# Converting a dense layer's float64 weights in place on ScalarE and VectorE

## The chip, the core and the metric

One core of a Trainium2 chip runs the kernel. The metric is the device time of one execution in microseconds (us), taken as the median of several runs. The engines are TensorE (PE, with its weight loads as PEld), VectorE (DVE), ScalarE (ACT), GpSimd (POOL) and SyncE (SP), which here only issues transfers.

## What is computed

Chunked attention with memory rows feeds a dense layer with a SiLU gate, and that feeds a routed layer of eight experts. The dense layer's weights are the part that the change touches. They are drawn without a cast, so they are float64, unlike q, k and v.

```python
def _moe_setup():
    n_tokens, d_model, d_ff = (3072, 512, 2048)
    return {'x': ..., 'w_in': np.random.randn(d_model, d_ff) * (1.0 / np.sqrt(d_model)), 'w_out': np.random.randn(d_ff, d_model) * (1.0 / np.sqrt(d_ff))}

def reference(**kwargs):
    attn_out = _attn_ref(**attn_kwargs)      # 4 batches, 8 heads, 768 rows, chunks of 32 with context
    x = np.ascontiguousarray(attn_out.transpose(0, 2, 1, 3)).reshape(B * S, H * D)
    h = x @ w_in                             # _moe_ref
    x = ((h * (1.0 / (1.0 + np.exp(-h)))) @ w_out).astype(np.float32)
    return _moe2_ref(x=x, **moe2_kwargs)     # gate, argmax expert, relu MLP of that expert
```

## The kernel before

The 3072 tokens are cut into 8 blocks j of 384; each is fed by four attention blocks n of 96 queries. The hidden width 2048 of the dense layer is cut into 16 slices f of 128. For each (j, f) TensorE forms `h{j}.{f}` (12 matmuls: three float32r passes over four column groups) and `y{j}.{f}` (9 matmuls: three passes for three groups of 128 tokens); between them ScalarE and VectorE do tanh, a multiplication, and a split into a high and a low part (`th`, `ts`, `gh`, `gl`; lines 558 to 561). The products of all f of block 0 come first, then block 1, and so on; `in_turn` keeps the order h, h, y, h, y.

The weights of a slice f are needed first by `h0.{f}`. So block 0 runs only as fast as slices are converted; from block 1 on the converted weights `wh` and `wl` (32 tiles of one pool tag "w" with 36 slots) stay in SBUF and are used again.

`conversion(f)` makes, for i = 0 (a slice of w_in) and i = 1 (a slice of w_out), from float64 words a float32 value and then two float32r parts. Each float64 is two 32-bit words, here called low and high. The units, with the engine that runs them:

- `c0_f` (SP, lines 467 and 469): the two loads into `wd{f}.0` and `wd{f}.1`. The w_in slice is 128 columns out of 2048, so each piece is 1 KB long in memory; those of w_out are 4 KB. It waits for `cb` of three slices before (`CONV_AHEAD`).
- `c1` (ACT; DVE for f = 0; lines 474, 476): high word, read as a float32, times 2^-112, into `wm`.
- `ca` (DVE, line 480): `wm` shifted left by three bits, both halves in one instruction of 1024 elements.
- `cs` (DVE, line 484): the sign of the high word put into `wm`.
- `cb` (DVE for f = 0, 3, ..., 15, line 489; else ACT, line 491): the top three bits of the low word, as an integer, into `wt`.
- `cl` (POOL, line 495): `wm` plus `wt`; this is the float32 value.
- `ch` (ACT, line 498): high part into `wh`.
- `c5` (line 502): `wm` minus `wh` into `wl`, on POOL for i = 0 and on DVE for i = 1.

All units are put in order once, when the program is built, by the list schedule of class `Plan`, from estimated lengths, ranks and free slots. On the chip each engine, and SP's queue of transfers, runs its own list strictly in that order and waits where something isn't there yet. So a load on SP that waits also holds back the loads of attention (`LQ`, `LK`, `LV`; lines 353, 359 to 361, 364) behind it.

Attention of the next blocks runs in between: scores `S` (PE, line 388), minima `M` (DVE, line 393), exponentials `E` (ACT, line 400), row sums and reciprocals `R` (DVE, lines 405 and 406), normalisation `N` (POOL, line 411, two instructions for each block n), transposes `X` (PE, line 415), copies `P` (line 418), values `V` (PE, line 423), and the split `H` and `L` (ACT line 426, DVE line 429). `h1.0` needs `L4` to `L7`.

Of the kernel before, what the change touches and what calls it, by code (L numbers as in the profile page):

```python
# [164 lines left out]
def kernel(  # L165
# [291 lines left out]
    def conversion(f):  # L457
        for i in range(2):
            T.new(f"wd{f}.{i}", "w", [P, DM, 2], I32)
        T.new(f"wm{f}", "w", [P, 2, DM])  # L460
# [3 lines left out]
        wd = [f"wd{f}.0", f"wd{f}.1"]

        def load():
            sp.dma_start(
                out=T[wd[0]].rearrange("p (c f) w -> p c (f w)", c=KD), in_=w_in[:, f * P:f * P + P].bitcast(I32).rearrange("(c p) x -> p c x", p=P))
            sp.dma_start(out=T[wd[1]].rearrange("p f w -> p (f w)"), in_=w_out[f * P:f * P + P, :].bitcast(I32))

        def scale_down(i):
            m, x = T[f"wm{f}"][:, i], T[wd[i]][:, :, 1].bitcast(F32)
            if f in D_C1:
                dve.tensor_scalar(out=m, in0=x, scalar1=2.0 ** -112, scalar2=None, op0=ALU.mult)
            else:
                act.activation(out=m, in_=x, func=AF.Copy, scale=2.0 ** -112)  # L476

        def shift():
            mi = T[f"wm{f}"].bitcast(I32)
            dve.tensor_scalar(out=mi, in0=mi, scalar1=3, scalar2=None, op0=ALU.logical_shift_left)  # L480
# [5 lines left out]
        def rest(i):
            t, x = T[f"wt{f}"][:, i], T[wd[i]][:, :, 0].bitcast(U32)
            if f in D_T1:
                dve.tensor_scalar(out=t, in0=x, scalar1=2.0 ** -29, scalar2=None, op0=ALU.mult)
            else:  # L490
                act.activation(out=t, in_=x, func=AF.Copy, scale=2.0 ** -29)
# [684 lines left out]
```

## Time and profile before

| what | value |
|---|---|
| three timed runs | 1021.09, 1023.49, 1030.64 us |
| their median | 1023.49 us |
| span of the profiled execution (first to last instruction) | 1021.5 us |
| time of the profiled execution outside its span | not recorded |
| PE busy, share of the span | 959.6 us, 94% |
| DVE / ACT / POOL busy | 724.1 / 479.0 / 218.2 us |
| moved by the DMA engines | 110.99 MB |

The profile lists an engine as busy while one of its instructions runs; neighbouring instructions of an engine can overlap by a few hundredths of a microsecond. A wait inside an instruction for something that is no semaphore is counted as its duration. The granted clock is a share of TensorE's 2.4 GHz.

### The profile page before, as it was taken

To read this page: it belongs to the slowest core of one execution; us is meant where nothing else is said; L and a number is where in the kernel's file an instruction comes from. 1 tells how busy PE (TensorE), PEld (TensorE's weight loads), DVE (VectorE), ACT (ScalarE), POOL (GpSimd) and SP (SyncE) were. 2 spreads that over 40 slices of the span, in tenths; PEclk is the share of its full clock that TensorE was granted. 3 is DMA by queue.
4 is the path that set the end of the run, shared out by engine and by line. 5 is a ranking of instruction groups with operands and counts; after the bars stand their busy time and mean duration, and the time that the engine had idled before them with its cause. 6 is when DMAs were issued, how large, how long until landed. Compare 5 with 4: busy or idle time off the path is not lost. (4 is left out here: it accounts for less than half of the span.)

```text
span 1021.5 us, 15964 instructions
## 1 busy us (share of the span) xinstructions
PE 959.6 (94%) x5356; PEld 847.6 (83%) x5356; DVE 724.1 (71%) x2031; ACT 479.0 (47%) x1273; POOL 218.2 (21%) x186
## 2 busy tenths in 40 slices
PE   6696899999999999999999999998999999999994
PEld 3575778889889889889889888997998888988983
DVE  5999988957966975984993993775975455544550
ACT  5666665626535544544553452224233344433541
POOL 6678552101201201111120210001012021112101
PEclk8789989999999999999999999999999999999998
DMA  9825421221231230221321211136057455456311
GB/s 285 271 77 169 132 70 50 89 90 50 78 101 30 82 117 20 81 89 42 99 72 59 88 43 42 42 101 218 22 179 232 153 169 176 138 163 208 129 49 44
DMA packets 99458, 110.99 MB, mean 109 GB/s; under 512 B 18623, under 2 KB 73695, under 8 KB 99360
## 3 DMA queue, kind: packets, MB, share of 16 engines
q1 hardware_dynamic: 95360, 96.96, 30.0%
q0 software_dynamic: 4000, 12.85, 3.8%
q8 instruction: 46, 0.75, 0.3%
q14 instruction: 52, 0.43, 0.1%
HBM read 97.20 MB, written 12.85 MB: 108 GB/s over the span
## 5 line engine op out<-in xcount | busy, mean ns | idle before, releaser
L411 POOL TENSOR_TENSOR pt<-pt,rs 96x512 f32<-96x512 f32 x64 | 83.8, 1328 | 411.7 <-DVE rs L406 332.3
L400 ACT ACTIVATE pt<-pt,mn 96x128 f32<-96x128 f32 x256 | 99.5, 392 | 42.6 <-DVE mn L393 42.5
L495 POOL TENSOR_TENSOR wm<-wm,wt 128x512 int32<-128x512 int32 x32 | 49.9, 1568 | 24.7 <-DVE wm L484 16.6
L400 ACT ACTIVATION_READ_ACCUMULATOR pt<-pt,mn 96x1 f32 x256 | 48.5, 190 | 0.0
L380 DVE TENSOR_TENSOR pad<-qk,pad 64x512 fp32r<-64x512 f32 x48 | 45.5, 947 | 0.7
L423 PE MATMUL pv<-px,v 128*64 128x96 f32 x512 | 30.9, 267 | 9.0 <-DVE mn L393 5.6
L423 PEld LDWEIGHTS pv<-px,v 128*64 128x64 f32 x512 | 24.5, 147 | 16.5 <-issue 12.7
L376 ACT CAST pad<-qk 64x512 fp32r<-64x512 f32 x48 | 29.5, 614 | 0.8 <-DMA qk<-in_k_dram 0.3
L502 POOL TENSOR_TENSOR wl<-wm,wh 128x512 fp32r<-128x512 f32 x16 | 24.8, 1548 | 5.2 <-ACT wh L498 5.2
L426 ACT CAST xh<-pv 128x384 fp32r<-128x384 f32 x32 | 15.1, 474 | 17.7 <-PE pv L423 17.7
L498 ACT CAST wh<-wm 128x512 fp32r<-128x512 f32 x32 | 19.6, 618 | 7.0 <-POOL wm L495 7.0
L393 DVE DVE_READ_ACCUMULATOR2_ANT mn<- 96x1 f32 x256 | 20.2, 79 | 0.0
L502 DVE TENSOR_TENSOR wl<-wm,wh 128x512 fp32r<-128x512 f32 x16 | 19.3, 1208 | 0.5 <-ACT wh L498 0.5
L480 DVE TENSOR_SCALAR wm<-wm 128x1024 int32<-128x1024 int32 x16 | 17.1, 1069 | 1.3 <-ACT wm L476 1.3
L890 POOL DMA_INDIRECT xge0.0_7148<-yd,gie x1 | 1.2, 1174 | 77.7 <-DMA rawxe0.1_7118<-in_moe_w_dram 77.7
L429 DVE TENSOR_TENSOR xl<-pv,xh 128x384 fp32r<-128x384 f32 x32 | 17.4, 547 | 0.0
L380 DVE TENSOR_TENSOR qs<-qk,qs 128x384 fp32r<-128x384 f32 x24 | 16.4, 682 | 0.5
L592 DVE DVE_READ_ACCUMULATOR2_ANT lg<- 128x1 f32 x192 | 15.7, 82 | 0.0
L376 ACT CAST qs<-qk 128x384 fp32r<-128x384 f32 x24 | 12.3, 512 | 0.2
L405 DVE TENSOR_SCALAR rs<-sm 96x8 f32<-96x8 f32 x32 | 9.6, 299 | 1.2 <-ACT pt L400 1.2
L632 DVE TENSOR_SCALAR ya<-ya,rg 128x512 f32<-128x512 f32 x16 | 7.4, 501 | 0.2
L406 DVE RECIPROCAL rs<-rs 96x8 f32<-96x8 f32 x32 | 6.4, 199 | 1.1
(6397 smaller groups left out, 3218.5 us busy)
## 6 DMA issues: line engine op xcount, KB each, us to landing
v<-in_v_dram SPq DMA_DIRECT2D x32, 256.0 KB, 2.7
qk<-in_k_dram SPq DMA_DIRECT2D x24, 256.0 KB, 3.2
qk<-in_q_dram SPq DMA_DIRECT2D x24, 192.0 KB, 3.3
yd<-ya SPq DMA_DIRECT2D x16, 256.0 KB, 2.1
pad<-in_k_dram SPq DMA_DIRECT2D x16, 128.0 KB, 3.9
yd<-yb SPq DMA_DIRECT2D x8, 256.0 KB, 2.5
qs<-in_q_dram SPq DMA_DIRECT2D x8, 192.0 KB, 4.5
wd0.0_114<-in_moe_w_in_dram SPq DMA_DIRECT2D x1, 512.0 KB
```

What stands on the lines that cost most here:

```text
L376: act.copy(out=to[0], in_=x)
L380: dve.tensor_tensor(out=to[1], in0=x, in1=to[0].bitcast(F32), op=ALU.subtract)
L393: dve.tensor_tensor_reduce(out=T[f"pt{n}"][:, h, :], in0=T[f"sc{n}.{i // 2}"][:, h % 4, :], in1=mask, scale=-scale, scalar=3.0e38, op0=ALU ...
L400: act.activation(out=pt[:, h, :], in_=pt[:, h, :], func=AF.Exp, bias=T[f"mn{n}"][:, h:h + 1], scale=-1.0, accum_out=T[f"sm{n}"][:, h:h + 1])
L411: pool.tensor_tensor(out=pt[:, half, :], in0=pt[:, half, :], in1=bc(T[f"rs{n}"][:, half], [QB, 4, P]), op=ALU.mult)
L423: pe.matmul(T[f"pv{n}"][r:r + 64, h // 2, :], T[f"v{n}"][:, D * h:D * h + D], T[f"px{n}"][:, h, :], start=True, stop=True)
L429: dve.tensor_tensor(out=T[f"xl{j}"][:, :, cols], in0=T[f"pv{n}"], in1=T[f"xh{j}"][:, :, cols].bitcast(F32), op=ALU.subtract)
L480: dve.tensor_scalar(out=mi, in0=mi, scalar1=3, scalar2=None, op0=ALU.logical_shift_left)
L495: pool.tensor_tensor(out=mi, in0=mi, in1=T[f"wt{f}"][:, i], op=ALU.add)
L498: (dve.tensor_copy if f in D_CH else act.copy)(out=T[f"wh{f}"][:, i], in_=T[f"wm{f}"][:, i])
L502: e.tensor_tensor(out=T[f"wl{f}"][:, i], in0=T[f"wm{f}"][:, i], in1=T[f"wh{f}"][:, i].bitcast(F32), op=ALU.subtract)
L592: dve.tensor_tensor_reduce(out=part(products), in0=part(y_at[t]), in1=T[f"wg{j}.{e // 2}"][:, e % 2], scale=1.0, scalar=0.0, op0=ALU.mult, ...
```

## The change

The host lays both weights out so that slice f is one block of 128 partitions with 4 KB each, contiguous. The load of a slice is two units now, one for each i, and each waits for `cv` of the same i three slices before. The intermediate tiles `wm` and `wt` are gone; everything up to the float32 value happens inside `wd`, seen as four 16-bit pieces per float64 (0 and 1 of the low word, 2 and 3 of the high word):

- `ct` (DVE for f = 0, 3, ..., 15, else ACT): top three bits of the low word into piece 0, as a 16-bit integer;
- `cs` (DVE): the sign bit of piece 3 into piece 1, 16 bits wide;
- `c1` (ACT, always): high word times 2^-112, in place;
- `cv` (DVE): high word shifted left by three, or'ed with the low word, in place; this is the float32 value;
- `ch` (ACT): high part into `wh`, as before;
- `c5` (DVE, always): the low part into `wl`.

```diff
-D_T1 = range(0, 16, 3)
-D_LO = [(f, 1) for f in range(16)]
-D_C1 = (0,)
-D_CH = ()
+D_T = range(0, 16, 3)
...
-        T.new(f"wm{f}", "w", [P, 2, DM])
-        T.new(f"wt{f}", "w", [P, 2, DM], I32)
...
+        def load(i):
+            sp.dma_start(out=T[f"wd{f}.{i}"].rearrange("p f w -> p (f w)"), in_=(w_in, w_out)[i][f].bitcast(I32))
+        def halves(i):
+            return T[f"wd{f}.{i}"].bitcast(U16)
+        def rest(i):
+            to, x = halves(i)[:, :, 0], T[f"wd{f}.{i}"][:, :, 0].bitcast(U32)
+            if f in D_T:
+                dve.tensor_scalar(out=to, in0=x, scalar1=2.0 ** -29, scalar2=7.0, op0=ALU.mult, op1=ALU.min)
             else:
+                act.activation(out=to, in_=x, func=AF.Copy, scale=7.49 * 2.0 ** -32)
         def sign(i):
+            x = halves(i)
+            dve.tensor_scalar(out=x[:, :, 1], in0=x[:, :, 3], scalar1=2 ** 15, scalar2=None, op0=ALU.bitwise_and)
+        def exponent(i):
+            x = T[f"wd{f}.{i}"][:, :, 1].bitcast(F32)
+            act.activation(out=x, in_=x, func=AF.Copy, scale=2.0 ** -112)
         def whole(i):
-            mi = T[f"wm{f}"][:, i].bitcast(I32)
-            pool.tensor_tensor(out=mi, in0=mi, in1=T[f"wt{f}"][:, i], op=ALU.add)
+            x = T[f"wd{f}.{i}"]
+            dve.scalar_tensor_tensor(out=x[:, :, 1], in0=x[:, :, 1], scalar=3, in1=x[:, :, 0], op0=ALU.logical_shift_left, op1=ALU.bitwise_or)
         def low(i):
-            e = dve if (f, i) in D_LO else pool
-            e.tensor_tensor(out=T[f"wl{f}"][:, i], in0=T[f"wm{f}"][:, i], in1=T[f"wh{f}"][:, i].bitcast(F32), op=ALU.subtract)
+            dve.tensor_tensor(out=T[f"wl{f}"][:, i], in0=T[f"wd{f}.{i}"][:, :, 1].bitcast(F32), in1=T[f"wh{f}"][:, i].bitcast(F32), op=ALU.subtract)
...
-        U(f"c0_{f}", "SP", 2920, load, [f"cb_{f - CONV_AHEAD}.1" if f < KF - 2 else f"c5_{f - 2}.1", f"c0_{f - 1}"], wd, extra=DMA_LAG)
+            U(f"c0_{x}", "SP", 400, lambda i=i: load(i), [f"cv_{f - CONV_AHEAD}.{i}", f"c0_{f}.0" if i else f"c0_{f - 1}.1"], [wd], extra=DMA_LAG)
+            U(f"cs_{x}", "DVE", 370, lambda i=i: sign(i), [f"ct_{x}"], [wd], **C)
+            U(f"c1_{x}", "ACT", 600, lambda i=i: exponent(i), [f"cs_{x}"], [wd], **C)
+            U(f"ct_{x}", *(("DVE", 370) if f in D_T else ("ACT", 600)), lambda i=i: rest(i), [f"c0_{x}"], [wd], **C)
+            U(f"cv_{x}", "DVE", 610, lambda i=i: whole(i), [f"c1_{x}", f"ct_{x}"], [wd], **C)
+            U(f"ch_{x}", "ACT", 560, lambda i=i: high(i), [f"cv_{x}"], [wd, f"wh{f}"], **C)
+            U(f"c5_{x}", "DVE", 610, lambda i=i: low(i), [f"ch_{x}"], [wd, f"wh{f}", f"wl{f}"], **C)
...
+    if name == "moe_w_in":
+        return a.reshape(-1, P, a.shape[1] // P, P).transpose(2, 1, 0, 3).reshape(-1, P, a.shape[0])
+    if name == "moe_w_out":
+        return a.reshape(-1, P, a.shape[1])
```

## Rows read from the trace of the kernel before

**Rows 1.** The page, part 1: busy time, share of span, instructions by engine.

```profile
PE 959.6 (94%) x5356; PEld 847.6 (83%) x5356; DVE 724.1 (71%) x2031; ACT 479.0 (47%) x1273; POOL 218.2 (21%) x186
```

**Rows 2.** Windows: length, busy of each engine, granted clock, DMA share, GB/s.

```profile
200.00:300.00 100.00, 99.26 (x601) 88.53 (x601) 75.81 (x245) 47.20 (x137) 12.55 (x10) 1.00 0.24 77
...
39.10:151.10 112.00, 91.15 (x461) 76.05 (x460) 106.95 (x196) 73.18 (x192) 80.18 (x56) 0.91 0.42 132
8.40:147.00 138.60, 105.51 (x563) 86.07 (x564) 131.78 (x277) 92.74 (x258) 97.89 (x70) 0.86 0.53 166
0.00:39.10 39.10, 25.06 (x145) 16.61 (x145) 28.02 (x101) 24.51 (x85) 24.15 (x31) 0.78 0.91 273
```

**Rows 3.** Waits of PE, 39 to 151 us: total, times, longest.

```profile
PE yp0.0_506 L529 <- DVE gl0.5_799 L561: 3.4, 1, 3.4
```

**Rows 4.** Timeline of PE: start, length, first matmuls of h0.0 and of h1.0.

```profile
39.09 1.10 PE L521 MATMUL hp0.0_439<-xh,wh 128*128 128x384 f32 x4
...
151.15 0.86 PE L521 MATMUL hp1.0_1461<-xh,wh 128*128 128x384 f32 x4
```

**Rows 5.** Windows, 0 to 150, of lines 480, 484, 489, 502 in turn.

```profile
0.00:150.00 150.00, 17.10 (x16) 0.87 0.55 168
...
0.00:150.00 150.00, 37.61 (x32) 0.87 0.55 168
...
0.00:150.00 150.00, 7.66 (x12) 0.87 0.55 168
...
0.00:150.00 150.00, 19.33 (x16) 24.76 (x16) 0.87 0.55 168
```

**Rows 6.** The same of lines 561 and 405, both DVE.

```profile
0.00:150.00 150.00, 15.02 (x15) 0.87 0.55 168
...
0.00:150.00 150.00, 5.73 (x8) 0.87 0.55 168
```

**Rows 7.** The same of lines 495 and 411, both POOL.

```profile
0.00:150.00 150.00, 49.93 (x32) 0.87 0.55 168
...
0.00:150.00 150.00, 20.83 (x16) 0.87 0.55 168
```

**Rows 8.** Timeline of DVE: instructions of the shortest lengths that recur.

```profile
11.90 0.42 DVE L474 TENSOR_SCALAR wm<-wd0.0_114 128x512 f32<-128x512 f32 x1
12.24 0.42 DVE L474 TENSOR_SCALAR wm<-wd0.1_116 128x512 f32<-128x512 f32 x1
...
51.55 0.68 DVE L484 SCALAR_TENSOR_TENSOR wm<-wd4.0_371,wm 128x512 int32<-128x512 int32 x1
52.15 0.68 DVE L484 SCALAR_TENSOR_TENSOR wm<-wd4.1_373,wm 128x512 int32<-128x512 int32 x1
...
53.82 0.68 DVE L480 TENSOR_SCALAR wm<-wm 128x1024 int32<-128x1024 int32 x1
...
14.26 0.17 DVE L405 TENSOR_SCALAR rs<-sm 96x8 f32<-96x8 f32 x1
```

**Rows 9.** Timelines of DVE, then of POOL: instructions that ran side by side.

```profile
21.52 2.23 DVE L405 TENSOR_SCALAR rs<-sm 96x8 f32<-96x8 f32 x1
...
39.46 1.78 DVE L502 TENSOR_TENSOR wl<-wm,wh 128x512 fp32r<-128x512 f32 x1
...
22.46 1.26 POOL L495 TENSOR_TENSOR wm<-wm,wt 128x512 int32<-128x512 int32 x1
...
39.07 3.32 POOL L495 TENSOR_TENSOR wm<-wm,wt 128x512 int32<-128x512 int32 x2 [0.68 <-issue]
```

**Rows 10.** Windows, 0 to 150, of line 491, ACT.

```profile
0.00:150.00 150.00, 12.87 (x20) 0.87 0.55 168
```

**Rows 11.** Timeline of SP's queue: transfers issued.

```profile
49.13 0.46 SPq L469 DMA_DIRECT2D wd9.1_702<-in_moe_w_out_dram  x1
...
73.47 0.33 SPq L353 DMA_DIRECT2D qs<-in_q_dram  x1
73.91 0.38 SPq L467 DMA_DIRECT2D wd10.0_789<-in_moe_w_in_dram  x1
```

**Rows 12.** Timeline of DVE: the last split that h1.0 needs.

```profile
143.53 0.55 DVE L429 TENSOR_TENSOR xl<-pv,xh 128x384 fp32r<-128x384 f32 x1
```

More of the change, by code (lines that the diff above doesn't have):

```diff
@@ L13 @@
 I32 = mybir.dt.int32
+U16 = mybir.dt.uint16
 U32 = mybir.dt.uint32
@@ L187 @@
     NT, DM = out.shape
-    DFF = w_in.shape[1]
+    KF = w_in.shape[0]
     E, _, FE = w1.shape
     NMOD = m_bias.shape[0]
-    KF = DFF // P
     KE = FE // P
@@ L459, in conversion @@
             T.new(f"wd{f}.{i}", "w", [P, DM, 2], I32)
-        T.new(f"wm{f}", "w", [P, 2, DM])
-        T.new(f"wt{f}", "w", [P, 2, DM], I32)
         T.new(f"wh{f}", "w", [P, 2, DM], F32R)
         T.new(f"wl{f}", "w", [P, 2, DM], F32R)
[L464 to L474, printed above, removed]
-            else:
[L476 to L480, printed above, removed]
+        def load(i):
+            sp.dma_start(out=T[f"wd{f}.{i}"].rearrange("p f w -> p (f w)"), in_=(w_in, w_out)[i][f].bitcast(I32))
@@ L482, in sign @@
+        def halves(i):
[4 more added lines that the diff above has]
+                dve.tensor_scalar(out=to, in0=x, scalar1=2.0 ** -29, scalar2=7.0, op0=ALU.mult, op1=ALU.min)
+            else:
+                act.activation(out=to, in_=x, func=AF.Copy, scale=7.49 * 2.0 ** -32)
         def sign(i):
-            mi = T[f"wm{f}"][:, i].bitcast(I32)
-            dve.scalar_tensor_tensor(out=mi, in0=T[wd[i]][:, :, 1], scalar=-2 ** 31, in1=mi, op0=ALU.bitwise_and, op1=ALU.bitwise_or)
@@ L486, in rest @@
[L486 to L491, printed above, removed]
+            x = halves(i)
[3 more added lines that the diff above has]
+            act.activation(out=x, in_=x, func=AF.Copy, scale=2.0 ** -112)
@@ L493, in whole @@
         def whole(i):
-            mi = T[f"wm{f}"][:, i].bitcast(I32)
-            pool.tensor_tensor(out=mi, in0=mi, in1=T[f"wt{f}"][:, i], op=ALU.add)
+            x = T[f"wd{f}.{i}"]
+            dve.scalar_tensor_tensor(out=x[:, :, 1], in0=x[:, :, 1], scalar=3, in1=x[:, :, 0], op0=ALU.logical_shift_left, op1=ALU.bitwise_or)
         def high(i):
-            (dve.tensor_copy if f in D_CH else act.copy)(out=T[f"wh{f}"][:, i], in_=T[f"wm{f}"][:, i])
+            act.copy(out=T[f"wh{f}"][:, i], in_=T[f"wd{f}.{i}"][:, :, 1].bitcast(F32))
@@ L506, in conversion @@
         for i in range(2):
-            U(f"c1_{f}.{i}", *(("DVE", 335) if f in D_C1 else ("ACT", 520)), lambda i=i: scale_down(i), [f"c0_{f}"], [wd[i], f"wm{f}"], **C)
-        U(f"ca_{f}", "DVE", 600, shift, [f"c1_{f}.0", f"c1_{f}.1"], [f"wm{f}"], **C)
-        for i in range(2):
-            U(f"cb_{f}.{i}", *(("DVE", 335) if f in D_T1 else ("ACT", 520)), lambda i=i: rest(i), [f"c0_{f}"], [wd[i], f"wt{f}"], **C)
-            U(f"cs_{f}.{i}", "DVE", 602, lambda i=i: sign(i), [f"ca_{f}"], [wd[i], f"wm{f}"], **C)
-            U(f"cl_{f}.{i}", "Pool", 1225, lambda i=i: whole(i), [f"cs_{f}.{i}", f"cb_{f}.{i}"], [f"wt{f}", f"wm{f}"], **C)
-            U(f"ch_{f}.{i}", *(("DVE", 335) if f in D_CH else ("ACT", 520)), lambda i=i: high(i), [f"cl_{f}.{i}"], [f"wm{f}", f"wh{f}"], **C)
-            U(f"c5_{f}.{i}", *(("DVE", 602) if (f, i) in D_LO else ("Pool", 1225)), lambda i=i: low(i), [f"ch_{f}.{i}"], [f"wm{f}", f"wh{f}", f"wl{f}"], **C)
+            x, wd = f"{f}.{i}", f"wd{f}.{i}"
@@ L1077 @@
         experts([("e", i) for i in range(N_FIRST)] + [("b", i) for i in range(N_BIG)] + [("s", i) for i in range(N_SMALL)])
-        first = ["LQ0", "LK0", "mk", "LQ1", "LK1", "c0_0", "ident", "LV0", "c0_1", "LQ2", "LK2", "LV1", "c0_2", "LQ3", "LK3", "LV2", "c0_3", "LV3"]
+        first = ["LQ0", "LK0", "mk", "LQ1", "LK1", "c0_0.0", "c0_0.1", "ident", "LV0", "c0_1.0", "c0_1.1", "LQ2", "LK2", "LV1", "c0_2.0", "c0_2.1", "LQ3", "LK3", "LV2", "c0_3.0", "c0_3.1", "LV3"]
         for i, n in enumerate(first):
```

## The prediction

> **What bounds the kernel now.** I read the page first: PE is busy for 94% of the span [rows 1], so only time in which PE stands still or runs below full clock can be won. The windows say where that is. From 200 to 300 us PE is busy for 99.26 of 100 us at granted clock 1.00, and the other engines have room [rows 2]; I take this window for the stages behind it. Before h1.0, which starts at 151.15 [rows 4], it is otherwise: from the first product h0.0 at 39.09 to h1.0, PE is busy for 91.15 of 112.0 us at a mean granted clock of 0.91, while DVE is busy for 106.95 of them [rows 2]. The waits of PE in that stretch name DVE's split `gl` as the releaser of the longest but one, 3.4 us [rows 3]. So block 0 is bound by VectorE, and whatever h1.0 gains there the whole program gains, since PE is full behind it.
>
> The next question is what fills DVE. The sums by line say: the conversion takes 17.10, 37.61, 7.66 and 19.33 us on DVE (lines 480, 484, 489, 502) [rows 5]. The timeline says that these are not the lengths of the work: instructions of 128x512 with two inputs recur at 0.68 us, and so does line 480's, a 32-bit `tensor_scalar` with 8-byte steps at 0.42 [rows 8]; but a line 502 takes 1.78 us, and a line 405 of eight elements takes 2.23 where 0.17 is usual [rows 8, 9]. The 2.23 us end at 23.75, and POOL's addition beside them ends at 22.46 + 1.26 = 23.72. The 1.78 us begin at 39.46 inside the first of two POOL additions (39.07, 3.32 us for both, so about 1.66 each); that one ends near 40.7, and 0.6 us later DVE is done [rows 9]. I read this as DVE held until POOL's instruction ends. The dearest thing about POOL's share is what it does to DVE.
>
> **What goes.** POOL's 32 additions (49.93 us, [rows 7]) and 16 subtractions (24.76 us, second number of the last of [rows 5]). POOL keeps the normalisation of attention, 16 instructions and 20.83 us [rows 7]. How much of DVE's time is stretch: line 480 has 17.10 - 16 x 0.68 = 6.2; line 484 37.61 - 32 x 0.68 = 15.9; line 489 7.66 - 12 x 0.42 = 2.6; line 502 19.33 - 16 x 0.68 = 8.4 [rows 5, 8]. Of the others, `gl` has 15.02 - 15 x 0.55 = 6.8 (0.55 is the 128x384 `tensor_tensor` of [rows 12]) and line 405 5.73 - 8 x 0.17 = 4.4 [rows 6, 8]. Together 44.3 us, beside 49.93 + 24.76 + 20.83 = 95.5 us of POOL work, or 0.46 us for each. If what stays on POOL stretches DVE at the same rate, 20.83 x 0.46 = 9.7 us stay and 34.6 us go.
>
> **What comes to DVE.** Neighbours overlap by 0.08 us, so one instruction moves the queue on by 0.60 us (51.55 to 52.15) or 0.34 (11.90 to 12.24) [rows 8]. Of the 0.60 kind there were 16 + 32 + 16 = 64 (`ca`, `cs`, half of `c5`), and there are 64 again (32 `cv`, 32 `c5`). Of the 0.34 kind there were 12 `cb` and 2 `c1`; now there are 32 `cs` and 12 `ct`, 30 more, which is 10.2 us if 16-bit pieces at 8-byte steps run like 32-bit words at 8-byte steps. No row shows a 16-bit instruction of this shape. From above I bound it by the 0.60 of the two-input kind: 44 x 0.26 = 11.4 us more. From below the shortest row is line 405's 0.17 [rows 8], at most 44 x 0.25 = 11 us less. I take 0.34, the row of the same operation, same step and same number of elements.
>
> On this one term the Trainium skill has a rule (VectorE: DVE Perf Modes, section "What auto-detection actually checks"): an instruction with a single source goes through both ports at two elements per cycle if source and destination are in SBUF and the outermost counts are even, while packing of two 16-bit values needs a step of one. By that rule the new `cs` and `ct` keep the two-port rate, my 10.2 us stand, and neither bound is reached; the 0.42 us row [rows 8] fits it for 32-bit words.
>
> **The sum.** DVE has its first work at 8.4 and its last `c5` near 147.0; it is busy for 131.78 of these 138.6 us [rows 2], so 6.8 us are idle. New busy time: 131.8 - 34.6 + 10.2 = 107.4. Idle time will grow: ACT and PE are then nearly as full as DVE, and six steps of a slice alternate between DVE and ACT. I take 10 us. The last `c5` comes at 8.4 + 107.4 + 10 = 125.8, which is 21.2 earlier, and h1.0 follows it as before, 4.2 us later (147.0 to 151.15). The span becomes 1021.5 - 21.2 = 1000.3. The median of the timed runs lies 2.0 above the span of the profiled execution, whose time outside the span isn't known; with that, 1002.3.
>
> **Priced at nothing, and their cover.** ScalarE: 30 + 20 + 32 conversions become 32 + 20 + 32; at 12.87 / 20 = 0.64 us [rows 10] that is 1.3 us on an engine busy for 73.18 of 112 us [rows 2]. In a stage of about 91 us it would be 82% full, so the cover is thin. If its 20 writes of 16 bits cost double, 12.9 us, ACT would hold 87 of 91 us and bound the stage; that belongs to the first rival. Transfers: 32 loads before and after. Longer pieces can help only up to 39.1 us, where DMA is 91% busy; later its share is 0.42 [rows 2]. From below the worth is nothing; from above, the three MB of w_in among about 10.7 MB moved by then (273 GB/s for 39.1 us) are 28% of them, or 10 us, more than the wait of the first h0.0 for DVE and PE would let through. I take nothing. The waits of the loads move from `cb` to `cv`, two steps later; behind a waiting load on SP's queue stand LQ, LK and LV, for which attention waits. The queue already has such holes: w_out's slice 9 goes out at 49.13, and slice 10 at 73.91, behind the LQ at 73.47 [rows 11]. A slice takes some 5 to 6 us in the new stage and the loads run three slices ahead, which hides the two steps. Four tiles of "w" per slice in place of six only ease this.
>
> **Rivals.** *Half of it.* 16-bit instructions at one element per cycle (11.4 us back), or ACT and DVE waiting for each other for 20 us and not 10, or ACT slowed by its 16-bit writes: the lead falls to about 10, and the time is 1012 to 1013; smaller doses of each give 1009 to 1016. For it: three engines near 85% in fixed orders. Against: the row of the same step.
>
> *Attention caps it.* h1.0 needs the last split of block 7, which ends at 143.53 + 0.55 = 144.1 [rows 12], only 7.1 us before h1.0. If attention of blocks 4 to 7 keeps its pace because its loads hang behind waiting ones, no more than 7.1 us come out: 1016.4. Against it: those blocks wait in DVE's queue too, and this queue gets shorter.
>
> *PE caps it from the other side.* 91.15 x 0.91 is 83 us of work at full clock, so h1.0 can't come before 39.1 + 83 = 122.1 unless h0.0 comes earlier: at most 29.1 won, 994.4; with an earlier h0.0 some 990.
>
> *Slower.* The long DVE instructions are not POOL's doing but that of something that stays (ScalarE's or the transfers' traffic on the same tiles). Then no stretch goes and DVE keeps the 10.2 us: 1033.7. It decides if less than 10.2 of the 44.3 us are given back. The ends that agree to 0.03 us in [rows 9] speak against it.
>
> **Chances.** The forecast, 14 to 29 us won, 994 to 1009: 0.60. Half of it, 1009 to 1016: 0.22. Attention's cap, 1016 and above but not slower: 0.08. Beyond 29 us: 0.05. Slower: 0.05. One per cent of the median, 10.2 us, is about what a measurement of this kernel can tell from no change; that is 1013.3. Faster then is 0.60 + 0.05 + about two thirds of 0.22 = 0.80; within 1% 0.15; slower 0.05. From 990 to 1015 lie the forecast, most of the half gain and most of the better case, some 0.84.
>
> **What would show it.** In the profile after: in-place `cv` and `c5` near 0.68 us except beside the normalisation, where POOL keeps some 20 us; `cs` near 0.42 (0.68 would be the first rival); h1.0 near 130; PE's waits for `gl` mostly gone and its granted clock between h0.0 and h1.0 above 0.91; from h1.0 to the end the same length as before. It would be wrong if `cv` still took 1.2 us on average with POOL idle, if `c1` or `ct` on ACT took over a microsecond, or if the time after h1.0 grew.

## The result, and the profile after

The changed kernel takes 1008.87 us (median of 4 runs, 1004.9 to 1010.27) where the kernel before took 1023.13 in the same series: a ratio of 0.9847, 95% interval 0.9804 to 0.9889. It is faster by 1.5%, inside the predicted range of 990 to 1015 and 6.9 us above the predicted 1002. The profiled execution has a span of 1008.4 us and took 1010.27, the slowest of the four.

First the page's part 1 (busy time, share of the span, instructions); it answers to [rows 1].

```profile
PE 956.8 (95%) x5356; PEld 844.1 (84%) x5356; DVE 705.6 (70%) x2061; ACT 492.3 (49%) x1275; POOL 146.7 (15%) x138
```

POOL has lost 48 instructions. ACT is busy for 13 us more than before although it got only two more instructions: that is the first sign of something that the prediction did not count on.

The windows (columns as in [rows 2]: stretch, length, busy time of PE, PEld, DVE, ACT and POOL, granted clock, DMA share, GB/s) of the start, of h0.0 to h1.0, of DVE's first work to its last `c5`, and of a stretch behind:

```profile
0.00:36.41 36.41, 23.24 (x144) 14.87 (x144) 21.70 (x98) 23.30 (x79) 14.77 (x24) 0.91 0.85 263
36.41:135.08 98.67, 87.72 (x459) 73.10 (x460) 91.97 (x217) 85.73 (x187) 18.35 (x14) 0.93 0.49 163
8.40:126.45 118.05, 95.38 (x537) 77.04 (x537) 109.57 (x305) 106.98 (x260) 26.69 (x22) 0.91 0.58 191
200.00:300.00 100.00, 99.30 (x588) 88.98 (x588) 70.31 (x232) 46.16 (x139) 10.51 (x8) 1.00 0.22 69
```

The stretch from h0.0 to h1.0 is 98.7 us long where it was 112.0 [rows 2], and h0.0 itself comes 2.7 us earlier. In the third row DVE is busy for 93% of the time and ACT for 91%: two engines are now nearly full where one was. In the last row PE is as full as before, so the gain lies ahead of it.

The sums from 0 to 150 us of the lines of the conversion, in turn L472 (`ct` on DVE), L474 (`ct` on ACT), L478 (`cs`), L486 (`cv`) and L492 (`c5`), answer to [rows 5]; the one number behind the length is the engine's busy time with these instructions alone:

```profile
0.00:150.00 150.00, 8.99 (x12) 0.93 0.54 174
0.00:150.00 150.00, 26.80 (x20) 0.93 0.54 174
0.00:150.00 150.00, 23.49 (x32) 0.93 0.54 174
0.00:150.00 150.00, 25.91 (x32) 0.93 0.54 174
0.00:150.00 150.00, 23.37 (x32) 0.93 0.54 174
```

`c5` takes 23.37 / 32 = 0.73 us and `cv` 0.81, where the two-input steps of the kernel before took 1.2 [rows 5]. But `cs` takes 0.73 and `ct` 0.75, not the 0.42 expected, and ScalarE's `ct` takes 1.34 us, twice the 0.64 of [rows 10]. The timeline of DVE shows both kinds side by side; the last row is POOL's at that time:

```profile
59.92 0.84 DVE L472 TENSOR_SCALAR wd6.1_535<-wd6.1_535 128x512 uint16<-128x512 uint32 x1
60.51 0.84 DVE L478 TENSOR_SCALAR wd7.0_562<-wd7.0_562 128x512 uint16<-128x512 uint16 x1
61.10 0.82 DVE L478 TENSOR_SCALAR wd6.1_535<-wd6.1_535 128x512 uint16<-128x512 uint16 x1
61.69 0.24 DVE L402 TENSOR_SCALAR rs<-sm 96x8 f32<-96x8 f32 x1
63.12 1.06 DVE L486 SCALAR_TENSOR_TENSOR wd6.0_499<-wd6.0_499 128x512 int32<-128x512 int32 x1
64.11 1.52 DVE L486 SCALAR_TENSOR_TENSOR wd6.1_535<-wd6.1_535 128x512 int32<-128x512 int32 x1
...
62.32 2.76 POOL L408 TENSOR_TENSOR pt<-pt,rs 96x512 f32<-96x512 f32 x2 [31.71 <-DVE rs L403]
```

The steps with 16-bit output move the queue on by 0.59 us (59.92 to 60.51, 60.51 to 61.10), not by 0.34. The eight-element line, here L402, takes 0.24 us and not 2.23 [rows 9]. The two long `cv` run beside POOL's normalisation (L408, 62.32 to 65.08): where POOL still works, DVE is still stretched.

Where h1.0's lead comes from is read from PE's own busy time up to h1.0, with as many matmuls in both (603). The first row is the kernel before's, the second the changed kernel's:

```profile
0.00:151.15 151.15, 116.26 (x603) 92.67 (x604) 135.02 (x296) 97.75 (x276) 104.33 (x86) 0.88 0.55 169
0.00:135.08 135.08, 110.96 (x603) 87.97 (x604) 113.67 (x314) 109.03 (x265) 33.12 (x38) 0.92 0.59 190
```

Of the 16.07 us, 10.8 are less standing still (151.15 - 116.26 = 34.9 us before, 24.1 after) and 5.3 are shorter matmuls: the mean granted clock rose from 0.88 to 0.92.

Last, how h1.0 stands to the last `c5` (timelines, first of DVE, then of PE):

```profile
124.18 0.69 DVE L492 TENSOR_TENSOR wl<-wd15.0_1110,wh 128x512 fp32r<-128x512 f32 x1
...
125.72 0.68 DVE L492 TENSOR_TENSOR wl<-wd15.1_1152,wh 128x512 fp32r<-128x512 f32 x1
...
129.54 0.86 PE L510 MATMUL hp0.15_1347<-xh,wh 128*128 128x384 f32 x4
...
133.71 0.85 PE L385 MATMUL sc8.0_1376<-pad,qs 128*96 128x256 f32 x6
134.40 0.84 PE L385 MATMUL sc8.1_1383<-pad,qs 128*96 128x256 f32 x6
135.08 0.51 PE L510 MATMUL hp1.0_1390<-xh,wh 128*128 128x384 f32 x2
```

The last `c5` ends at 126.4, but h0.15, the first product of the last slice, starts at 129.54, 3.1 us later; in the kernel before it started with the end of the last `c5`. Then two score products of block 8, which the kernel before had done ahead of h0.15, take another 1.4 us. So h1.0 comes 8.7 us after the last `c5`, not 4.2. Neither product waits for that instruction: it makes the w_out half of `wl`, which only y0.15 reads, behind h1.0. The half that h0.15 reads is ready at 124.87 (first row), and from 120.07 on PE works without a gap: it is PE that is behind, by 4.7 us.

### The profile page after: what moved, and what is told of

Read it like the earlier page. It is cut to its first block, busy times and chain, and to the rows that moved or that the text cites. A ratio compares the mean times of both kernels' runs of the same rounds, so it can differ in the third digit from the quotient of the medians.

```text
span 1008.4 us, 15917 instructions
## 1 busy us (share of the span) xinstructions
PE 956.8 (95%) x5356; PEld 844.1 (84%) x5356; DVE 705.6 (70%) x2061; ACT 492.3 (49%) x1275; POOL 146.7 (15%) x138
## 5 line engine op out<-in xcount | busy, mean ns | idle before, releaser
L408 POOL TENSOR_TENSOR pt<-pt,rs 96x512 f32<-96x512 f32 x64 | 87.3, 1383 | 498.4 <-DVE rs L403 406.8
L420 PE MATMUL pv<-px,v 128*64 128x96 f32 x512 | 28.0, 252 | 1.4 <-issue 1.4
L420 PEld LDWEIGHTS pv<-px,v 128*64 128x64 f32 x512 | 22.2, 136 | 8.2 <-issue 7.4
L472 DVE TENSOR_SCALAR wd0.0_114<-wd0.0_114 128x512 uint16<-128x512 uint32 x1 | 0.7, 733 | 9.5 <-DMA wd0.0_114<-in_moe_w_in_dram 9.5
L663 DVE TENSOR_SCALAR rej<-rows,rj 128x24 f32<-128x24 f32 x24 | 7.1, 294 | 0.0
L652 DVE CAST rpf<-ri 128x3 f32<-128x3 int32 x8 | 6.1, 768 | 0.2
L654 DVE TENSOR_TENSOR rj<-rk,rpf 128x3 f32<-128x3 f32 x8 | 5.4, 679 | 0.0
```

The costliest lines, as they stand in the source:

```text
L408: pool.tensor_tensor(out=pt[:, half, :], in0=pt[:, half, :], in1=bc(T[f"rs{n}"][:, half], [QB, 4, P]), op=ALU.mult)
L420: pe.matmul(T[f"pv{n}"][r:r + 64, h // 2, :], T[f"v{n}"][:, D * h:D * h + D], T[f"px{n}"][:, h, :], start=True, stop=True)
L663: dve.tensor_scalar(out=ej, in0=iota_j, scalar1=T[f"rj{j}"][:, t:t + 1], scalar2=tok1[:, i:i + 1], op0=ALU.is_equal, op1=ALU.mult)
```

## The experiments

In the table, h1.0 is the start of the first product of block 1; it, the last `c5` and the span are those of the one profiled execution, whose time is not always near the median (that of after_ct32 is the shortest of its five, that of the changed kernel the longest of its four). Times are medians, ratios are to the kernel before as timed in the same series.

| kernel | last `c5` ends | h1.0 | span | us | ratio, 95% interval |
|---|---|---|---|---|---|
| before | 146.9 | 151.15 | 1021.5 | 1023.13 | |
| before_plan | 147.8 | 152.55 | 1023.8 | 1025.81 | 1.0016 (0.9992 to 1.004) |
| before_layout | 147.0 | 151.27 | 1018.7 | 1022.31 | 0.999 (0.9975 to 1.0005) |
| before_no_pool | 131.6 | 135.68 | 1007.6 | 1010.64 | 0.988 (0.9863 to 0.9896) |
| changed | 126.4 | 135.08 | 1008.4 | 1008.87 | 0.9847 (0.9804 to 0.9889) |
| after_pool_low | 133.1 | 139.41 | 1010.9 | 1010.41 | 0.9878 (0.9844 to 0.9911) |
| after_ct32 | 119.4 | 128.06 | 998.6 | 1005.15 | 0.9818 (0.9798 to 0.9837) |
| after_plan | 123.7 | 129.11 | 999.8 | 1002.00 | 0.98 (0.9765 to 0.9835) |
| ct32_dve | 134.8 | 140.26 | 1011.1 | 1013.02 | 0.991 (0.9878 to 0.9942) |
| ct32_act | 122.2 | 128.30 | 999.1 | 1000.45 | 0.9785 (0.9745 to 0.9825) |
| ct32_plan | 120.8 | 127.40 | 999.0 | 1003.62 | 0.9807 (0.9767 to 0.9846) |
| ct32_act_plan | 119.3 | 125.02 | 995.9 | 997.19 | 0.9743 (0.9701 to 0.9785) |
| ct32_act_plan_masks | 118.6 | 124.43 | 995.8 | 998.70 | 0.9749 (0.9706 to 0.9792) |

### Only the engine changes: before_no_pool

```
-            pool.tensor_tensor(out=mi, in0=mi, in1=T[f"wt{f}"][:, i], op=ALU.add)
+            dve.tensor_tensor(out=mi, in0=mi, in1=T[f"wt{f}"][:, i], op=ALU.add)
-D_LO = [(f, 1) for f in range(16)]
+D_LO = [(f, i) for f in range(16) for i in range(2)]
```

(and the plan's unit "Pool", 1225 becomes "DVE", 602)

> The kernel before, with its tiles, its layout and its order of steps, but the 48 conversion instructions that GpSimd has (line 495, 32 of them, and the 16 of line 502 on POOL) given to VectorE; the unit lengths in the plan follow. Only the engine changes. Theory A, VectorE's instructions are stretched by GpSimd's work: VectorE gets 48 x 0.60 = 28.8 us more and loses the stretch of 74.7 us of GpSimd work, 34.6 us by the 0.46 us per us of the prediction: VectorE's busy time to 150 falls by about 6 us, instructions of lines 480, 484 and 489 take their shortest lengths (0.68, 0.68, 0.42 us) nearly all the time, the whole takes 1013 to 1025 us. Rival B, the stretch has another cause (ScalarE, loads): VectorE's instructions stay as long as they were, its busy time grows by 29 us or more, the whole takes 1045 to 1055 us.

Measured: 1010.64 us. The sums from 0 to 150 us of lines 480 and 484, both DVE, and the window up to the last `c5`:

```profile
0.00:150.00 150.00, 10.77 (x16) 0.92 0.57 173
0.00:150.00 150.00, 24.02 (x32) 0.92 0.57 173
8.40:131.62 123.22, 102.34 (x562) 81.55 (x561) 118.94 (x324) 93.91 (x259) 27.15 (x22) 0.90 0.60 183
```

Lines 480 and 484, untouched, fall from 17.10 and 37.61 us [rows 5] to 10.77 and 24.02, close to 16 x 0.68 and 32 x 0.68. VectorE does 48 instructions more and is busy for 118.94 us, not 131.78 [rows 2]. With 28.8 us of new work, 131.78 + 28.8 - 118.94 = 41.6 us went. Rival B falls. Theory A had the cause but not the size: VectorE's busy time fell by 12.8 us and not by 6, and 1010.64 lies below its range of 1013 to 1025. And this edit alone brings most of what the change brought: 0.988 against 0.9847, with intervals that overlap, and h1.0 within 0.6 us. The rest of the change, the in-place form with its two fewer tiles and fewer steps, can't be told from nothing by these times.

### Only the layout: before_layout

```
-            sp.dma_start(out=..., in_=w_in[:, f * P:f * P + P].bitcast(I32).rearrange("(c p) x -> p c x", p=P))
-            sp.dma_start(out=..., in_=w_out[f * P:f * P + P, :].bitcast(I32))
+            for i in range(2):
+                sp.dma_start(out=T[wd[i]].rearrange("p f w -> p (f w)"), in_=(w_in, w_out)[i][f].bitcast(I32))
```

(and the host's layout of both weights, as in the change)

> The kernel before with one part of the change alone: the float64 weights come in the layout that is contiguous per partition (two loads for each slice, 4 KB in one piece per partition in each). Theory A, loads set nothing between 39 and 147 us: 1020 to 1026 us, the end of the conversion moves by less than 2 us, the start (first slice) may come up to 2 us earlier. Rival B, a good part of the 14 us that the change brought is the layout's (fewer pieces, less transfer time beside the others): 1016 us or less and the last instruction of line 502 at 143 us or earlier.

Measured: 1022.31 us, a ratio of 0.999 (0.9975 to 1.0005), and h1.0 at its old place, 151.27. The transfers were rightly priced at nothing, as far as the layout goes; the move of the loads' waits from `cb` to `cv` was not tested by itself.

### The forms by themselves: micro_forms

```
+    for _ in range(2):
+        for i in range(4):
+            dve.tensor_scalar(out=h[i][:, :, 1], in0=h[i][:, :, 3], scalar1=2 ** 15, scalar2=None, op0=ALU.bitwise_and)
```

(and so for each form; `h` is a tile of 64-bit words seen as four 16-bit pieces; this kernel leaves out all that the reference computes)

> Computes nothing of the reference: eleven forms of the conversion's instructions, eight of each, alone on VectorE, then alone on ScalarE, 128 x 512 elements, with no other engine at work; the output rows are then filled from one of the tiles. Theory A (16 bits at a step of 8 bytes run at one element per cycle on VectorE; 16-bit output at that step costs ScalarE double): VectorE's 16-bit forms at a step of 8 bytes take about 0.53 us from one to the next, the contiguous 16-bit form about 0.2, the 32-bit single-source forms about 0.34; ScalarE's 16-bit-output form 1.1, its other forms 0.56. Rival B (the forms run at the prediction's 0.34, and other work in the kernel stretched them): 0.34 for VectorE's strided 16-bit forms too, and 0.56 for ScalarE's 16-bit output.

The timeline of DVE and then of ACT; each row is eight instructions, so the distance from one row's start to the next's, divided by eight, is the step. L98 writes 32 bits contiguous, L101 32 bits at 8-byte steps, L104 and L107 16 bits at 8-byte steps, L110 reads 16 bits at 8-byte steps and writes them contiguous, L113 is contiguous on both sides, L116 is `cv`:

```profile
9.41 2.71 DVE L98 TENSOR_SCALAR y<-x 128x512 int32<-128x512 uint32 x8
12.03 2.77 DVE L101 TENSOR_SCALAR x<-x 128x512 int32<-128x512 uint32 x8
14.72 4.70 DVE L104 TENSOR_SCALAR x<-x 128x512 uint16<-128x512 uint32 x8
19.20 4.77 DVE L107 TENSOR_SCALAR x<-x 128x512 uint16<-128x512 uint16 x8
23.75 2.81 DVE L110 TENSOR_SCALAR z<-x 128x512 uint16<-128x512 uint16 x8
26.47 1.71 DVE L113 TENSOR_SCALAR q<-z 128x512 uint16<-128x512 uint16 x8
28.09 4.91 DVE L116 SCALAR_TENSOR_TENSOR x<-x 128x512 int32<-128x512 int32 x8
...
32.43 3.90 ACT L122 ACTIVATE x<-x 128x512 int32<-128x512 uint32 x7
36.23 9.26 ACT L125 ACTIVATE x<-x 128x512 uint16<-128x512 uint32 x8
45.22 3.94 ACT L128 ACTIVATE x<-x 128x512 f32<-128x512 f32 x7
```

On DVE: 0.33 and 0.34 us with 32 bits, contiguous or not; 0.56 and 0.57 with 16 bits written at 8-byte steps; 0.34 with 16 bits read at 8-byte steps and written contiguous; 0.20 contiguous on both sides. On ACT: 3.80 / 7 = 0.54 with 32 bits written at 8-byte steps, 8.99 / 8 = 1.12 with 16 bits. Up to 22.29 us no other engine worked, so for VectorE's forms of L98 to L104 and most of L107 it isn't contention. ScalarE's rows ran beside transfers of the output; the last step of its 16-bit form, after these had ended, is as long as the others (1.13 us, 42.96 to 44.09). It is the write of 16 bits at a step that costs, on both engines; on VectorE a read of 16 bits at that step (0.34) costs no more than one of 32.

### The first step writes 32 bits: after_ct32

```
-            to, x = halves(i)[:, :, 0], T[f"wd{f}.{i}"][:, :, 0].bitcast(U32)
+            to, x = T[f"wd{f}.{i}"][:, :, 0], T[f"wd{f}.{i}"][:, :, 0].bitcast(U32)
```

> The changed kernel with one edit: the first step (ct) writes its whole number as 32 bits over the low word, not as 16 bits; the sign goes into that word's upper half afterwards as before. Both forms, VectorE's 12 and ScalarE's 20. Theory A, the 16-bit output is what made this step dear (ScalarE's 20 at 1.34 us against 0.67 with 32 bits in the kernel before, VectorE's 12 at 0.75 against 0.42), and ScalarE sets the end of the conversion together with VectorE: ScalarE's steps fall by about 11 us and VectorE's by 2 to 3, the last instruction of line 492 ends 3 to 8 us earlier than at 126.4, the whole takes 1001 to 1006 us. Rival B, only VectorE sets the end: it ends 2 to 3 us earlier and the whole takes 1005 to 1008 us. Rival C, TensorE's own work sets it from 36 us on: the conversion ends earlier, the first product of block 1 does not, and the whole stays at 1007 to 1010 us.

Measured: 1005.15 us, 1000.91 in the profiled execution; the last `c5` ends 7.0 us earlier and h1.0 comes 7.0 us earlier, 2.6 of them there already at h0.0 (33.81 against 36.41). The sum of L474 (ACT, 0 to 150 us) and the window up to the last `c5`:

```profile
0.00:150.00 150.00, 13.32 (x20) 0.95 0.54 176
8.40:119.41 111.01, 92.60 (x536) 73.84 (x537) 105.88 (x304) 96.14 (x260) 26.69 (x22) 0.94 0.62 203
```

ScalarE's `ct` halved, from 26.80 to 13.32 us, ACT's busy time fell by 10.8 and DVE's by 3.7. The end moved by more than DVE's 3.7: DVE's idle time shrank too, from 118.05 - 109.57 = 8.5 to 5.1 us. That is theory A; by B the end would have come 2 to 3 us earlier, and by C h1.0 would have stayed. The median alone would not tell A (1001 to 1006) from B (1005 to 1008).

### Half of POOL's share back: after_pool_low

```
-            dve.tensor_tensor(out=T[f"wl{f}"][:, i], in0=..., op=ALU.subtract)
+            (dve if i else pool).tensor_tensor(out=T[f"wl{f}"][:, i], in0=..., op=ALU.subtract)
```

> The changed kernel with 16 of the 32 instructions of line 492 (the low part of the first weight matrix) back on GpSimd, as the kernel before had them; the plan's length follows. Theory A, GpSimd's instructions cost VectorE in stretch about what they save it: VectorE gives away 16 x 0.60 = 9.6 us and gets back 0.46 us for each of 24.8 us of GpSimd work, 11.4 us: its busy time to 150 changes by -1 to +4 us, the whole by 0 to +4 us against the changed kernel (a ratio of 0.985 to 0.990 to the kernel before). Rival B, the stretch was of the 32 adds of line 495 alone, or of some other cause: VectorE is freed of 9.6 us and the whole falls by 4 to 9 us (0.976 to 0.981).

Measured: 1010.41 us, 0.9878 (0.9844 to 0.9911), 1.5 us above the changed kernel and not to be told from it. The sums from 0 to 150 us of L472, L478, L486, L492 (here DVE's, then POOL's) and L550 (`gl`):

```profile
0.00:150.00 150.00, 9.90 (x12) 0.92 0.53 171
0.00:150.00 150.00, 25.52 (x32) 0.92 0.53 171
0.00:150.00 150.00, 27.43 (x32) 0.92 0.53 171
0.00:150.00 150.00, 15.17 (x16) 24.99 (x16) 0.92 0.53 171
0.00:150.00 150.00, 14.20 (x18) 0.92 0.53 171
```

VectorE gave away 9.6 us. It got back 0.9 on L472 (9.90 against 8.99), 2.0 on L478 (25.52 against 23.49) and 1.5 on L486. Over the unstretched lengths, L492 has 15.17 - 16 x 0.68 = 4.3 where the changed kernel has 23.37 - 32 x 0.68 = 1.6, and `gl` has 14.20 - 18 x 0.55 = 4.3 where it has 11.24 - 19 x 0.55 = 0.8. Together 10.6 us, as theory A says: what POOL takes over it takes back.

### The plan's lengths: after_plan and before_plan

```
-            U(f"cs_{x}", "DVE", 370, ...
+            U(f"cs_{x}", "DVE", 560, ...
-            U(f"ct_{x}", *(("DVE", 370) if f in D_T else ("ACT", 600)), ...
+            U(f"ct_{x}", *(("DVE", 560) if f in D_T else ("ACT", 1120)), ...
```

> The changed kernel with the same instructions; only the lengths that its plan takes for the two steps with 16-bit output are those measured (0.56 us on VectorE where it had 0.37, 1.12 on ScalarE where it had 0.60), so the order on the engines differs. Theory A, the work on ScalarE and VectorE is what sets the end (109.6 and 107.0 us of 118): order moves little, the whole within 2 us of the changed kernel, 1006 to 1011 us. Rival B, a part of the conversion's length is that the plan queued ScalarE's exponentials behind steps that ran twice as long as it thought: 1002 to 1006 us.

Measured: 1002.0 us (1000.77 to 1003.71, none of its times among those of the changed kernel): rival B. Beside its own runs of the kernel before that is 0.98, and the interval overlaps the changed kernel's a little (up to 0.9835, from 0.9804). The instructions are the same and DVE's busy time up to the last `c5` is the same:

```profile
8.40:123.72 115.32, 95.11 (x555) 77.37 (x554) 110.02 (x305) 106.21 (x261) 23.98 (x22) 0.94 0.59 196
```

109.57 us in the changed kernel, 110.02 here. Of the 6.0 us by which h1.0 comes earlier, 3.2 are there already at h0.0 (33.17 against 36.41). Seen from the other end they are 2.7 us of the last `c5` (idle time of DVE: 8.5 down to 5.3) and 3.3 us of h1.0's distance to it (8.7 down to 5.4). One place where it shows: in the changed kernel ACT does four `ct`, two `ch` and a `c1` from 103.3 on before block 7's exponentials (109.9) and `gh0.11`, and PE waits 3.4 us for that `gh`, its longest wait between 36 and 135 us; here the exponentials start at 104.5 and that wait is 0.4 us (the one for `gh0.0` grew from 1.0 to 3.7).

For the kernel before, the same was done with its own measured lengths (1.05 to 1.15 us for VectorE's steps where the plan had 0.60, 1.55 for GpSimd's where it had 1.225, and so on):

> The kernel before with the same instructions; only the plan's lengths of the conversion's steps are brought to those that its trace shows (on VectorE 1.05 and 1.12 us where it had 0.60, 1.15 where it had 0.60, 0.60 where it had 0.335; on GpSimd 1.56 and 1.55 where it had 1.225; on ScalarE 0.56 where it had 0.52). Theory A, VectorE has no idle time to win there (24.2 to 24.9 of 25 us from 25 to 125): 1019 to 1026 us. Rival B, a part of what the change brought is that it happened to be planned better, and the kernel before loses as much by its wrong lengths as the changed one did (6.9 us): 1013 to 1018 us.

Measured: 1025.81 us, 1.0016 (0.9992 to 1.004): nothing to win there, theory A. There were few gaps to fill: from 25 to 125 us VectorE idles for 1.6 us in the kernel before, for 3.7 in the changed kernel and for 1.6 in after_plan.

### Who has the first step: ct32_act and ct32_dve

```
-D_T = range(0, 16, 3)
+D_T = ()
```

is ct32_act, and with `range(16)` it is ct32_dve; both have the 32-bit step of after_ct32.

> The changed kernel with the first step writing 32 bits, and all 32 of these on ScalarE (12 were VectorE's). VectorE gets 12 x 0.34 = 4.1 us less, ScalarE 12 x 0.56 = 6.7 us more. Theory A, with 32 bits written VectorE is again the fuller one (24.6 to 24.9 of 25 us between 25 and 100 in the kernel that only wrote 32 bits, ScalarE 21.3 to 21.8) and sets the end: the first product of block 1 comes 1 to 4 us earlier than its 128.1, the whole takes 1001 to 1005 us. Rival B, ScalarE sets it with VectorE: it is back at 24 of 25 us, no change or up to 4 us slower, 1005 to 1009 us.

> The changed kernel with the first step writing 32 bits, and all 32 of these on VectorE (20 were ScalarE's). VectorE gets 20 x 0.34 = 6.8 us more, ScalarE 20 x 0.56 = 11.2 us less. Theory A, VectorE sets the end of the conversion: it comes 5 to 7 us later than in the kernel that only wrote 32 bits, h1.0 at 133 to 135, the whole takes 1009 to 1012 us. Rival B, ScalarE sets it: 2 to 8 us earlier, 997 to 1003 us. Rival C, TensorE sets it: no change, 1003 to 1007 us.

Measured: 1000.45 us with all of them on ScalarE, 1013.02 with all on VectorE. The windows up to the last `c5`, first ct32_act, then ct32_dve:

```profile
8.40:122.25 113.85, 95.32 (x555) 77.91 (x555) 103.41 (x293) 101.50 (x272) 23.59 (x22) 0.96 0.61 199
8.40:134.76 126.36, 104.75 (x554) 84.30 (x553) 116.63 (x326) 87.61 (x241) 22.71 (x22) 0.85 0.54 179
```

Both are to be compared with after_ct32. With ACT relieved to 87.61 of 126 us the conversion got longer: there VectorE's work sets the end (theory A). h1.0 moved by 12 us, not 5 to 7, but 5.8 of these are there already at h0.0 (39.57 against 33.81); from h0.0 to h1.0 it is 6.4.

The other way round it is not shown. VectorE's busy time fell by 2.5 us (103.41 against 105.88), but its idle time rose from 5.1 to 10.4, the last `c5` came 2.8 us later, and h1.0, expected 1 to 4 us earlier, did not move (128.30 against 128.06): relieved of work, VectorE waits for others. Rival B is not what is seen either: ScalarE has at most 23.6 of 25 us between 25 and 125, not 24, and the median, 1000.45, is below the ranges of both theories, 4.7 us below that of after_ct32. The profiled executions are not apart: 1001.01 us here, 1000.91 for after_ct32, whose five lie between that and 1006.79. So as far as the runs show the 4.7 us are spread and not a gain.

### Both together: ct32_plan, ct32_act_plan, ct32_act_plan_masks

> The changed kernel with the first step writing 32 bits (12 on VectorE, 20 on ScalarE), and with 0.56 us in the plan for the sign step, as measured, where it had 0.37. Theory A, the two gains (4 us of the 32 bits, 7 us of the plan) are for the most part one, the same idle time of VectorE and the same backlog of TensorE: VectorE was busy for 85.15 of 85.6 us already with the 32 bits alone, so no more than 3 us come: 1001 to 1006 us. Rival B, they add: 996 to 1000 us.

> As the kernel before this one, and all 32 of the first steps on ScalarE. VectorE has 4.1 us less work, and idled for 3.7 of 88.95 us with the old length. Theory A, the right length gives some of these 3.7 us back: 996 to 1000 us, VectorE 24.5 or more of 25 us from 60 to 120. Rival B, ScalarE (22 of 25 us there) or TensorE holds it: 999 to 1003 us, no change.

> As the one before, and the copy of the masks put first on VectorE, ahead of the first conversion step, behind whose load it and the first scores' minima stood (VectorE began at 10.7 us in the changed kernel). Theory A, the start sets the first product: it comes 1 to 3 us earlier and so does the end, 994 to 1000 us. Rival B, the first slices' loads set the first product and the early minima only take their place in the queue: within 2 us of the kernel without it.

The edits are those above, in the last kernel with

```
-        U("masks", "DVE", 270, ..., ["mk"], ["mk"])
+        U("masks", "DVE", 270, ..., ["mk"], ["mk"], boost=1.0e6)
```

Measured: 1003.62, 997.19 and 998.70 us. The 32-bit step and the right lengths do not add (theory A): each mostly fills the same gaps. With all first steps on ScalarE the right length brings 3.3 us more, in the median, in the profiled execution and at h1.0 (theory A), though the intervals overlap; the masks bring nothing (rival B). ct32_act_plan is the best version here, 0.9743 (0.9701 to 0.9785), and its interval lies below the changed kernel's:

```profile
8.40:119.30 110.90, 95.52 (x551) 78.67 (x551) 102.08 (x291) 99.72 (x271) 25.04 (x22) 0.92 0.61 203
```

Even here VectorE idles for 8.8 of 110.9 us; three engines at 86 to 92% in fixed orders seem to be about what this stage gives, but that was not tested further.

## Why the prediction was right where it was right, and wrong where it was wrong

**The bound, and what it is worth.** Right: the gain is all ahead of block 1, and PE from 200 to 300 us is as full as before. Not quite right is "whatever h1.0 gains there the whole program gains". h1.0 came 16.07 us earlier, but the last job's first product only 13.20 (992.77 to 979.57). Of the 2.9 us given back, 1.2 fall in block 1, which has 80.91 us where it had 79.69: one wait for `gl` of 0.6 us, and matmuls 0.5 us longer in sum. That does not come of the earlier h1.0: block 1 takes 80.8 to 81.0 us in every other version but before_layout, also in before_plan, whose h1.0 is at 152.55; why it was 79.7 in the kernel before is not shown. The other 1.7 us are not the change's as far as the runs show: after_ct32 has a lead of 23.1 us at h1.0 and of 23.2 at the last job, and before_layout, with no lead at h1.0, has 2.5 us there.

**The stretch.** Right in its cause: before_no_pool shows it by an edit of the engine alone, and after_pool_low shows it the other way round. The reading of [rows 9], that DVE is held until POOL's instruction ends, is what the Trainium skill says as well (SBUF — State Buffer, section "Who interferes with whom"): a VectorE instruction with two SBUF inputs, or in its two-port mode, and a GpSimd one that reads SBUF exclude each other for a whole instruction. The trace agrees: `c5` falls from 1.2 to 0.73 us once GpSimd is away. (The prediction's 0.6 us from the end of POOL's addition to that of DVE's 1.78 us is 0.54.) In size it was too small. By the subtraction used for before_no_pool, and with the new work below, 131.78 + 20.1 - 109.57 = 42.3 us went, where 34.6 were predicted; two instructions, about 1.1 us, are no longer ahead of the last `c5`, and lines 316 and 318 (the routing bias), which the prediction's list did not have, fell from 3.17 to 1.07 us with as many instructions. What stayed is 4.1 us on `cv` (25.91 - 32 x 0.68), 1.6 on `c5` and 0.8 on `gl`, 6.5 in all, and not 9.7; the small line 402 is back at its usual length. Why the rate fell below 0.46 us for each us of the normalisation is shown in part only. The 16-bit steps have no share in it: of the 32 `cs` one ran beside a GpSimd instruction, of the 12 `ct` none. But the hold goes both ways (timelines of POOL, then of DVE):

```profile
79.44 5.01 POOL L408 TENSOR_TENSOR pt<-pt,rs 96x512 f32<-96x512 f32 x2 [12.12 <-DVE rs L403]
...
80.82 0.68 DVE L486 SCALAR_TENSOR_TENSOR wd9.0_680<-wd9.0_680 128x512 int32<-128x512 int32 x1
```

Here a two-input step runs at its shortest length, and it is POOL that takes 5.01 us for two instructions, where two took 2.6 in the kernel before (20.83 / 16 each, [rows 7]).

**The 16-bit steps.** This is the term that failed. Each was priced at 0.34 us, the row of the 32-bit form, and the Trainium skill's rule (VectorE: DVE Perf Modes, section "What auto-detection actually checks") was cited for it: one source, both sides in SBUF, even counts, so two elements per cycle. The forms by themselves show 0.56 to 0.57 us for 16 bits written at 8-byte steps. The trace does not agree with the rule for this form; the rule holds for the 32-bit writes and for the 16-bit reads at that step (0.34). So 44 x 0.565 - 14 x 0.34 = 20.1 us came to VectorE, not 10.2, which is nearly the upper bound of the prediction (10.2 + 11.4).

**The sum.** Two errors of opposite sign, +9.9 on the 16-bit steps and about -7.7 on the stretch, left DVE's busy time at 109.57 where 107.4 was predicted. The idle time was 8.5 us where 10 was taken. So the last `c5` ends at 126.4, where 125.8 was predicted, for a reason that is half luck.

**"h1.0 follows it as before."** Wrong by 4.5 us (8.7 and not 4.2), and it was never a dependence, since h1.0 reads nothing that the last `c5` makes: h0.15 starts 3.1 us after that `c5` because PE is behind, and 1.4 us of block 8's scores stand in between. With the right lengths in the plan PE is not behind (after_plan: h0.15 starts at 123.36, before the last `c5` ends at 123.7). With the 0.6 us of the last `c5`, this step and the given-back 2.9 us are the difference between the predicted span, 1000.3, and the measured 1008.4: 0.6 + 4.5 + 2.9 = 8.0.

**ScalarE priced at nothing.** Wrong by what the prediction itself had named: its 20 writes of 16 bits cost double, 26.80 us and not 12.87 [rows 10]. It did not "bound the stage" alone, but at 91% it took away the slack: after_ct32, with ScalarE's 13.5 us back and 3.7 of VectorE's, ends the conversion 7.0 us earlier.

**Transfers priced at nothing.** Right for the layout: before_layout, 0.999.

**The rivals.** The time of the first, *half of it*, is 1009 to 1016, and 1008.87 lies at its edge: its two 16-bit doses were both there, and the larger stretch that went paid for them. *Attention's cap* did not come: the split of block 7 that h1.0 needs ends at 125.3, 9.8 us before h1.0. *PE's cap* is not reached, but PE's backlog is the beginning of it. *Slower* fell with before_no_pool.

**The signs.** `c5` and `cv` near 0.68: 0.73 and 0.81, never the 1.2 that would have been wrong. `cs` near 0.42: no, 0.73, and the prediction had said what that would mean. PE's waits for `gl` mostly gone: yes, ScalarE's `gh` is the longest now. Granted clock above 0.91 from h0.0 to h1.0: 0.93. h1.0 near 130: no, 135.08. Two of the three signs of being wrong came true: `ct` on ACT took over a microsecond (1.34), and the time after h1.0 grew, by 2.9 us (870.4 to 873.3).

Not settled is what limits the stage once VectorE is relieved (ct32_act), and what makes block 1 take 1.2 us more than in the kernel before.

## What to carry to other kernels

When a busy engine's instructions differ in length without a difference in their work, look for the engine that runs beside the long ones, and price an offload by what it does to its neighbour: here 9.6 us given to GpSimd cost VectorE 10.6. Price each instruction by the type and step that it writes, not by its element count, and measure a form of which the trace has no row. After a change of forms, bring the plan's lengths up to date before judging it: the same instructions in a better order were worth 6.9 us, nearly half as much again as the change itself, while in the kernel before, whose VectorE had fewer gaps, they were worth nothing.

## What the hardware showed that was not expected

- 16 bits written at 8-byte steps: 0.56 us from one to the next on VectorE (with no other engine at work) and 1.12 on ScalarE, for 128x512 elements; 32 bits at the same steps 0.34 and 0.54. The same 16 bits read at that step and written contiguous: 0.34 on VectorE.
- GpSimd holds VectorE's 16-bit steps too, though they have one input and take 0.57 us. In the changed kernel they hardly met (one `cs` of 32). In after_pool_low ten `cs` ran beside GpSimd, at 0.99 us on average, the other 22 at 0.76; one of the ten (timelines of POOL, then of DVE):

```profile
73.53 1.30 POOL L492 TENSOR_TENSOR wl<-wd7.0_575,wh 128x512 fp32r<-128x512 f32 x1 [2.98 <-issue]
...
73.64 1.80 DVE L478 TENSOR_SCALAR wd9.0_683<-wd9.0_683 128x512 uint16<-128x512 uint16 x1
```

  POOL ends at 74.83, and 0.61 us later `cs` is done.

- A third of h1.0's lead, 5.3 of 16.07 us, came from shorter matmuls: 110.96 us for the 603 that had taken 116.26. TensorE's clock has two levels, 1.2 and 2.4 GHz (granted 0.50 and 1.00). In the changed kernel it falls to the lower one after the wait for `gh0.11` (timeline of PE, then windows):

```profile
114.98 0.79 PE L516 MATMUL yp0.0_479<-wh,gh0.11_1209 128*128 128x512 f32 x1 [3.39 <-ACT gh0.11_1209 L549]
117.21 0.63 PE L517 MATMUL yp0.1_480<-wl,gh0.11_1209 128*128 128x512 f32 x1
123.76 0.39 PE L518 MATMUL yp0.0_479<-wh,gl0.12_1266 128*128 128x512 f32 x1
...
116.00:118.00 2.00, 2.00 (x5) 1.49 (x5) 2.00 (x5) 1.85 (x5) 2.00 (x1) 0.50 0.00 0
122.00:124.00 2.00, 2.00 (x23) 1.49 (x22) 1.97 (x4) 1.99 (x5) 0.00 (x0) 1.00 0.00 0
```

PE stood still for 3.39 us before 114.98. From 116 to 118 us the granted clock is 0.50, at full busy time, and a product of 128x512 takes 0.63 us; from 122 to 124 it is 1.00 and the product takes 0.39. So this wait cost more than its own length.
